# Attention and feed-forward on one core: other queues for the first loads, a table subtraction and some squares on GpSimd, other planned times

## The chip, the core and the metric

The kernel runs on one core of a Trainium2 chip. The metric is the device time of one execution in microseconds (us). A core has a matmul engine (TensorE, PE in the profile; its weight loads are PEld), an engine for elementwise work (VectorE, DVE), one for activation functions (ScalarE, ACT), GpSimd (POOL) and SyncE (SP). Each engine works through a queue of its own in order. DMAs are issued from the queues of SP, ACT or POOL.

## The reference, cut to what matters

```python
# attention: q, k, v are [8, 8, 576, 64]; bias_table is [32, 8]
scores = scale * np.matmul(q, k.transpose(0, 1, 3, 2)) + bias   # bias depends on |i - j| alone
attn = softmax(scores, axis=-1)
x = np.matmul(attn, v)            # -> [4608, 512], heads side by side
# feed-forward: w_in [512, 2048], w_out [2048, 512], alpha [2048]
h = x @ w_in
s = np.sin(alpha * h)
g = h + s * s / (alpha + 1e-09)
out = g @ w_out                   # [4608, 512]
```

## The kernel before

The work is staged by batch entry `t` (8 of them). For each `t` the heads are taken in four pairs `p`, in two groups `g` of two pairs. `plan_unit` makes a unit of scores on PE, then `exp` on ACT (line 646), and a multiplication by `exp(bias)` on DVE (lines 665 and 655), since `exp(s + b) = exp(s) exp(b)`. Far from the diagonal the bias is constant, so only a band is multiplied. `plan_av` multiplies with `v` on PE (a column of ones in `v` gives the sum of the row), DVE takes the reciprocal and normalises (lines 773 and 774), and the result is turned into `xT`.

Then comes the feed-forward on a block `b` of 512 rows, `plan_moe_in`. For each of 16 slices `f` of 128 columns: four matmuls for `h` (tag `h`, PSUM banks 0 to 5), `sin` on ACT (`sn`, line 837, into one of three buffers `s16`), the square (`sqr`, on ACT at line 844 or on another engine at line 846, into one of three buffers `sq`), and `g` on DVE (`gg`, line 851), which frees the bank of `h`. The `g` of a block are made in the order of `f`. `plan_mo` multiplies `g` by `w_out`.

The order in each engine's queue is made by a planner (`Plan`, lines 60 to 196), which runs while the program is built. A task has a cost for each engine that may take it, a priority, and an earliest time `nb`. The planner keeps one time per engine at which that engine is free, all set to `T_START` at first. At each step it finds the earliest start of each engine's candidates (line 152) and then emits, over all engines, the task with the smallest start, and among equal starts the one that ends first (line 166). A task that several engines may take thus goes where its planned start is earliest. The constants at lines 199 to 224 are what it knows of DMAs: `T_M2` and `T_MH` when the bias tables `m2r` and `mhr` may be used, `T_V` when `v` may be, `T_W` and `T_WO` when `w_in` and `w_out` may be, `T_EPS` when the product for the bias table may start. While a planned gap on PE before `WARM_END` is over 0.3 and bank 7 or 6 is free, it puts in a small matmul on zeros (`warm1`).

What is not planned is emitted in program order. Lines 467 to 499 are the opening. `tabN` (the bias table) has its last row `tabL` taken off on DVE (line 496), ACT makes `tabE = exp(tabN)`, and `plan_eps` (line 581) multiplies it with a constant on PE, copies the result to `e_sb` on DVE, and calls `loads()` in the same emission. `loads()` (line 501) emits, at once and in this order: on SP, the write of `e_sb` to `e_dram` and the loads of `v[0]`; on POOL, the reads of `m2r` and `mhr` back from `e_dram`, `w_in` mixed with the casts of `v[0]` to f16 (`cast_v`, lines 403 and 406), `q` and `k` of `t = 1`, `w_out`, the loads of `v[1]` (`v1st`), the staging of `q` and `k` of `t = 2`, and last `cast_v(1)`. No task of the plan of before has POOL among its engines, and the next POOL instruction after `cast_v(1)` is at line 378.

PSUM banks 6 and 7 serve the tags `av` and `mo`: results of `plan_av`, transposes of `q` and `k`, the product in `plan_eps`, the transpose of `alpha`, and the output blocks.

Of the kernel before, what the change touches and what calls it, by code (L numbers as in the profile page):

```python
# [13 lines left out]
ALU = mybir.AluOpType  # L14
# [186 lines left out]
QUOTA = 48  # L201
OFFSET = 0
T_START = 4.0
T_FIRST = (5.7, 6.0)
T_EPS = 6.5
T_PAIR = ((7.0, 7.6), (9.5, 11.5), (9.5, 11.5))
T_M2 = (13.0, 15.0, 17.0, 17.0)
T_MH = 14.5
T_B2 = 32.0
FILL_GAP = 0.2  # L210
NORM0 = 800
W2_PRI = 9640
SQ = {"ACT": 0.52, "DVE": 0.38}
T_V = (18.0, 52.0)
T_TR1 = (35.0, 36.5)
T_W = 29.0
T_WO = (40.0, 43.0, 46.0, 49.0)
WARM0 = 13
WARM_GAP = 0.3
# [19 lines left out]
def kernel(  # L239
# [11 lines left out]
    nc = tc.nc  # L251
    T, H, S, D = q.shape
# [48 lines left out]
    vst, vhst = [], []  # L301
# [11 lines left out]
    tabN = sgl.tile([NB, H], F32, name="tabN")  # L313
    tabL = sgl.tile([NB, H], F32, name="tabL")
# [49 lines left out]
    def stage_kq(t):  # L364
        for dst, src in ((staged_k, k), (staged_q, q)):
            nc.gpsimd.dma_start(
                out=dst.ap()[t].rearrange("s (h d) -> s h d", h=H),
                in_=src[t].rearrange("h s d -> s h d"),
            )
# [30 lines left out]
    def cast_v(t, eng, cs):  # L400
        for c in cs:
            if c < 4:
                eng.tensor_copy(out=vs[t][:, c, :, 0:D], in_=vst[t][:, c])
                continue
            z = c - 4
            eng.tensor_copy(
                out=vhs[t][64 * z : 64 * z + 64, :, VC * z : VC * z + D],
                in_=vhst[t][64 * z : 64 * z + 64],
            )

    def load_nat(dst, h0, h1, src, eng):

        eng.dma_start(out=dst, in_=src[h0:h1].rearrange("h (p i) d -> p h (i d)", i=SI))

    def load_w_in16(js):
        src = moe_w_in.rearrange("(j p) ff -> p j ff", p=128)
        for j in js:
            nc.gpsimd.dma_start(out=w_in16[:, j, :], in_=src[:, j, :])

    def load_w_out16():  # L420
        src = moe_w_out.rearrange("(f p) n -> p f n", p=128)
        for fh in range(4):
            nc.gpsimd.dma_start(
                out=w_out16[:, 4 * fh : 4 * fh + 4, :], in_=src[:, 4 * fh : 4 * fh + 4, :]
            )
# [25 lines left out]
    def load_m2r(eng, h0, h1):  # L451

        eng.dma_start(
            out=m2r[:, h0:h1],
            in_=bass.AP(tensor=e_dram, offset=EW * h0, ap=[[1, 128], [EW, h1 - h0], [1, XW]]),
        )

    def load_mhr(eng):
        for z in range(2):
            eng.dma_start(  # L460
                out=mhr[64 * z : 64 * z + 64],
                in_=bass.AP(tensor=e_dram, offset=EW * z + 192,
                            ap=[[1, 64], [2 * EW, NP], [1, 192]]),
            )

    P_ = nc.gpsimd
    P_.memset(id_sb, 1.0)
    P_.affine_select(
        out=id_sb, in_=id_sb, compare_op=ALU.is_equal, fill=0.0, base=0, pattern=[[-1, 128]],
# [6 lines left out]
        out=tabL,  # L476
        in_=bass.AP(tensor=bias_table.tensor, offset=bias_table.offset + (NB - 1) * H,
                    ap=[[0, NB], [1, H]]),
# [8 lines left out]
    vp = v[0].rearrange("h s d -> s h d")  # L487
    vq = v[0].rearrange("(hp two) s d -> two s hp d", two=2)
# [4 lines left out]
    x0 = nat0[:, 1].rearrange("s two (i d) -> s i two d", i=SI)  # L493
    nc.scalar.activation(out=natb[:, 1, :, 0], in_=x0[:, :, 0], func=AF.Copy)
    nc.vector.tensor_copy(out=natb[:, 1, :, 1], in_=x0[:, :, 1])
    nc.vector.tensor_tensor(out=tabN, in0=tabN, in1=tabL, op=ALU.subtract)
    nc.scalar.activation(out=tabE, in_=tabN, func=AF.Exp)
    warm(WARM0)
    clear(P_, 1)
# [1 line left out]
    def loads():  # L501

        nc.sync.dma_start(out=e_dram.ap(), in_=e_sb)
        for c in range(4):
            nc.sync.dma_start(out=vst[0][:, c], in_=vp[128 * c : 128 * c + 128])
        for z in range(2):
            nc.sync.dma_start(out=vhst[0][64 * z : 64 * z + 64], in_=vq[z, 512:S])
        load_m2r(P_, 0, 2)
        load_mhr(P_)
        load_m2r(P_, 2, 4)  # L510
        load_m2r(P_, 4, H)
        cast_v(0, P_, (0,))
        load_w_in16((0,))
        cast_v(0, P_, (1, 2))
        load_w_in16((1,))
        cast_v(0, P_, (3, 4, 5))
        load_w_in16((2, 3))
        for kq, src in ((0, k), (1, q)):
            load_nat(nat2[:, kq], 0, H, src[1], P_)
        load_w_out16()  # L520
        load_v32(1, P_)
        stage_kq(2)
        cast_v(1, P_, range(6))

    plan = Plan()
# [53 lines left out]
        return [x], [plan.add({"DVE": 0.25}, tail, [x], pri + 30)]  # L579

    def plan_eps():
        b, c = Buf("mo"), Cell()

        def mm(e):
            c.v = bank(b)
            full(c.v[0:H, 0:EW], tabE, phi_sb, True, True)

        def cp(e):
            copy_on(e, e_sb, c.v[0:H, 0:EW])
            loads()  # L590

        m = plan.add({"PE": 0.25}, mm, [], -900, nb=T_EPS, new=[b])
        plan.add({"DVE": 0.6}, cp, [m], -800, use=[b])

    def plan_alpha():
        b, c = Buf("mo"), Cell()
# [15 lines left out]
    def plan_unit(t, g, p, kind, c, u, ub, done, gate, base):  # L612
# [36 lines left out]
        x = plan.add({"ACT": n / 1200.0 + 0.065}, ex, [mark] + gate, base + 20, use=[b, ub])  # L649
        late = 0.0 if t else T_MH if kind == "C" else T_M2[p]  # L650
        if kind == "C":
# [87 lines left out]
    def plan_av(t, g, p, w, u, ub, done, base):  # L739
# [11 lines left out]
        for i, qc in enumerate(QS):  # L751

            def mm(e, i=i, qc=qc):
# [5 lines left out]
                for z in range(2):  # L759
                    for c in range(4):  # L760
# [4 lines left out]
            prev = [plan.add({"PE": 0.31}, mm, us + prev, base + AV_PRI + i,  # L765
                             nb=T_B2 if w == 2 else T_V[t] if t < 2 else 0.0, new=[ab] if i == 0 else [],
                             use=[ub] if i == 0 else [ub, ab])]
# [46 lines left out]
    def plan_moe_in(b, tbl):  # L814

        gcell[b], gbuf[b] = Cell(), Buf("g")
        xs = [d for (t, w), ds in xdone.items() for d in ds for q0, n in [(WIN if t else WIN0)[w]]
              if S * t + q0 < 512 * b + 512 and S * t + q0 + n > 512 * b]
        sins = []
        for f in range(NF):  # L820
            hb, sb, qb = Buf("h"), Buf("s16"), Buf("sq")
            h, s16, sq = Cell(), Cell(), Cell()

            def mm(e, f=f, h=h, hb=hb):
                h.v = bank(hb)
                x0 = 512 * b % XN
                m = min(512, XN - x0)
                for y, a, n in ((0, x0, m), (m, 0, 512 - m)):
                    if n == 0:
                        continue  # L830
                    for j in range(4):
                        full(h.v[:, y : y + n], w_in16[:, j, 128 * f : 128 * f + 128],
                             xT[:, j, a : a + n], j == 0, j == 3)

            def sn(e, f=f, h=h, s16=s16):
                s16.v = new_s16()
                nc.scalar.activation(  # L837
                    out=s16.v, in_=h.v, func=AF.Sin, scale=alphaT[:, f : f + 1]
                )

            def sqr(e, s16=s16, sq=sq):
                sq.v = new_sq()
                if e == "ACT":
                    nc.scalar.activation(out=sq.v, in_=s16.v, func=AF.Square)  # L844
                else:
                    k_of(e).tensor_tensor(out=sq.v, in0=s16.v, in1=s16.v, op=ALU.mult)  # L846

            def gg(e, f=f, h=h, sq=sq):
                if f == 0:
                    gcell[b].v = new_g()  # L850
                nc.vector.scalar_tensor_tensor(  # L851
                    out=gcell[b].v[:, f, :], in0=sq.v, scalar=inv_a[:, f : f + 1], in1=h.v,
                    op0=ALU.mult, op1=ALU.add,
                )
                if f == 0 and 1 <= b < T - 1:
                    nc.gpsimd.tensor_copy(out=tick, in_=gcell[b].v[0:1, 0, 0:1])
                    load_v16(b + 1)
                    if b + 2 < T:
                        stage_kq(b + 2)

            pri = PB + 10000 + 1000 * (b - (PB // 1000000)) + 10 * f
            m = plan.add({"PE": 4 * t_pe(512)}, mm, xs, pri, nb=T_W if b == 0 else 0.0, new=[hb])
            x = plan.add({"ACT": t_act(512) + 0.09}, sn, [m, al] + tbl, pri, new=[sb], use=[hb])
            y = plan.add(SQ, sqr, [x], pri - 5,
                         new=[qb], use=[sb])
            gdone[(b, f)] = plan.add({"DVE": 0.66}, gg, [y], pri - 6,
                                     after=[gdone[(b, f - 1)]] if f else [],
                                     new=[gbuf[b]] if f == 0 else [],
                                     use=[hb, qb] if f == 0 else [hb, qb, gbuf[b]])
            sins.append(x)  # L870
        return m, sins
# [35 lines left out]
    PB = 0  # L907
    tr = {(0, 0, kq): plan_tr(0, 0, kq, -1000, T_FIRST[kq]) for kq in range(2)}
    plan_eps()
    al = plan_alpha()  # L910
    gate, pe_gate = [], []
    for t in range(T):
# [29 lines left out]
        for b in [t] if t < T - 1 else [t, t + 1]:  # L942
            m, s_ = plan_moe_in(b, tbl)
# [36 lines left out]
```

## Time and profile before

| | us |
|---|---|
| median of three runs | 391.51 |
| lowest, highest run | 386.42, 392.5 |
| the profiled execution's own time | 388.48 |
| its span, first to last instruction | 386.7 |
| PE busy | 369.5 |
| ACT busy | 315.7 |
| DVE busy | 272.7 |
| POOL busy | 89.7 |

The profile is of one execution. Its timelines give the start of a piece of work, its length, the engine (a name that ends in q is a DMA issued from that engine's queue), the line, the operation, output and inputs, and in brackets how long the engine had stood idle before it and what released it. A line of a helper stands for all its callers: matmuls are all at line 437, copies on DVE at 535 and on ACT at 533. The 1.78 us between the span and the execution's time lie outside the profiled instructions.

### The profile page before, as it was taken

Reading aid. Unit: us, or ns where it says so; the run is one execution under the profiler, and the core shown is the slowest. Engines: PE = TensorE matmul, PEld = TensorE weight load, DVE = VectorE, ACT = ScalarE, POOL = GpSimd, SP = SyncE. Lnnn points to the kernel's source line nnn. Section 1 sums busy time; section 2 is a strip of 40 time slices with the busy share of each in tenths; the row PEclk is TensorE's granted clock in tenths of the full one; section 3 lists DMA queues with packets and bytes.
Section 4 is the critical chain, followed back from the end, with each engine's and each line's share of the span. In section 5 each row is a group of like instructions: output and inputs, shape, how many; then the busy total and the mean of one; then the engine's idle time right before and its main releaser. Section 6 shows DMA issues by size and latency. Waiting matters only on the chain.

```text
span 386.7 us, 8905 instructions
## 1 busy us (share of the span) xinstructions
PE 369.5 (96%) x3551; PEld 202.6 (52%) x3551; DVE 272.7 (71%) x614; ACT 315.7 (82%) x435; POOL 89.7 (23%) x116
## 2 busy tenths in 40 slices
PE   8568989999999999999999999999999999999995
PEld 3245544654466445686565446544667456444442
DVE  5476995759766886688677967696759676999000
ACT  4937998969997999879996999699979997998111
POOL 5773440009000280009000820073004100000000
PEclk9959999999999999999999999999999999999999
DMA  8999991289912699259915992399429812000112
GB/s 158 232 214 204 226 156 31 57 133 126 133 49 75 131 98 151 58 117 110 182 24 137 119 153 56 93 155 142 70 77 138 73 51 77 5 0 3 72 65 83
DMA packets 141946, 40.91 MB, mean 106 GB/s; under 512 B 131064, under 2 KB 136288, under 8 KB 141904
## 3 DMA queue, kind: packets, MB, share of 16 engines
q0 software_dynamic: 89904, 19.04, 55.3%
q1 hardware_dynamic: 51744, 21.00, 23.3%
q8 instruction: 28, 0.46, 0.5%
q10 hardware_dynamic: 256, 0.30, 0.3%
q14 instruction: 14, 0.11, 0.1%
HBM read 37.73 MB, written 16.52 MB: 140 GB/s over the span
## 4 chain that ended last, share of the span: by engine, by line
PE 88%; DVE 7%; DMA 3%; issue 1%; ACT 0%; DVEq 0%; ACTq 0%
PE pb L437 87%; DVE g L851 2%; DMA m2r<-e_dram 2%; DVE u L665 1%; DMA natx<-in_k_dram 1%; PE pb L798 1%; DMA e_dram<-e_sb 1%; DVE xn L774 1%; DVE kT L535 1%; DVE sq L846 1%; DVE kt L575 1%; ACT u L646 0%; DVE xT L535 0%; DVE rd L773 0%; DVE e_sb L535 0%
## 5 line engine op out<-in xcount | busy, mean ns | idle before, releaser
L646 ACT ACTIVATE u<-pb 128x1024 f16<-128x1024 f32 (+1 forms) x176 | 154.0, 966 | 15.9 <-PE pb L437 15.3
L437 PE MATMUL pb<-w_out,g 128*128 128x512 f16 x576 | 138.7, 380 | 0.0
L437 PE MATMUL pb<-xT,w_in 128*128 128x512 f16 (+4 forms) x704 | 128.0, 340 | 0.0
L837 ACT ACTIVATE s<-pb,alphaT 128x512 f16<-128x512 f32 x144 | 93.1, 681 | 14.7 <-PE pb L437 14.4
L851 DVE SCALAR_TENSOR_TENSOR g<-sq,inv_a,pb 128x512 f16<-128x512 f16 x144 | 101.5, 743 | 3.9 <-ACT sq L844 2.5
L437 PEld LDWEIGHTS <-w_in 128*128 128x128 f16 x704 | 64.0, 98 | 55.2
L665 DVE TENSOR_TENSOR u<-u,m2r 128x512 f16<-128x512 f16 (+1 forms) x128 | 61.8, 492 | 36.9 <-ACT u L646 31.3
L437 PEld LDWEIGHTS <-g 128*128 128x128 f16 x576 | 53.0, 98 | 61.4 <-issue 9.3
L437 PEld LDWEIGHTS <-u 128*128 128x128 f16 x1440 | 56.7, 99 | 16.4 <-DVE qT L535 5.2
L437 PE MATMUL pb<-v,u 128*128 128x65 f16 x1280 | 56.4, 195 | 0.0
L378 POOL COPY kt<-kT 64x256 f16<-64x256 f16 x12 | 5.5, 456 | 189.6 <-DMA kT<-staged_k 157.0
L437 PE MATMUL pb<-qT,kT 64*128 64x64 f16 (+1 forms) x512 | 43.1, 288 | 3.4 <-ACT u L646 2.6
L844 ACT ACTIVATE sq<-s 128x512 f16<-128x512 f16 x67 | 42.1, 628 | 1.1
L437 PE MATMUL pb<-vh,u 128*128 128x130 f16 x160 | 35.7, 223 | 4.9 <-DVE qT L535 4.9
L846 DVE TENSOR_TENSOR sq<-s 128x512 f16<-128x512 f16 x77 | 33.2, 436 | 10.0 <-ACT s L837 9.1
L774 DVE TENSOR_TENSOR xn<-pb,rd 128x384 f16<-128x384 f32 (+2 forms) x68 | 32.1, 471 | 2.3
L533 ACT ACTIVATE outs<-pb 128x512 f32<-128x512 f32 x15 | 9.0, 597 | 27.6 <-PE pb L437 27.6
L437 PEld LDWEIGHTS <-kT 64*128 64x128 f16 x512 | 17.0, 94 | 25.9 <-issue 18.5
L773 DVE RECIPROCAL rd<-pb 128x6 f32<-128x6 f32 (+2 forms) x68 | 12.6, 185 | 12.7 <-PE pb L437 11.6
L383 POOL DMA_DIRECT2D v<-in_v_dram x24 | 21.2, 897 | 0.1
L904 ACT ACT_TABLE_LOAD x15 | 19.2, 1283 | 0.3
L535 DVE COPY outs<-pb 128x512 f32<-128x512 f32 x21 | 14.5, 690 | 4.7 <-PE pb L437 4.7
(70 smaller groups left out, 159.5 us busy)
## 6 DMA issues: line engine op xcount, KB each, us to landing
out_dram<-outs SPq DMA_DIRECT2D x36, 256.0 KB, 2.2
staged_k<-in_k_dram POOLq DMA_DIRECT2D x6, 576.0 KB, 8.2
staged_q<-in_q_dram POOLq DMA_DIRECT2D x6, 576.0 KB, 11.2
v<-in_v_dram POOLq DMA_DIRECT2D x24, 128.0 KB, 4.9
w_in<-in_moe_w_in_dram POOLq DMA_DIRECT2D x4, 512.0 KB, 8.5
w_out<-in_moe_w_out_dram POOLq DMA_DIRECT2D x4, 512.0 KB, 18.9
w_out<-in_v_dram SPq DMA_DIRECT2D x4, 256.0 KB, 4.2
v1st<-in_v_dram POOLq DMA_DIRECT2D x4, 256.0 KB, 17.2
```

The source lines that it names most:

```text
L383: nc.gpsimd.dma_start(out=vs[t % 2][:, c, :, 0:D], in_=vp[128 * c : 128 * c + 128],)
L437: nc.tensor.matmul(out=out, lhsT=lhsT, rhs=rhs, start=start, stop=stop)
L535: k_of(e).tensor_copy(out=o, in_=i)
L646: nc.scalar.activation(out=o, in_=x, func=AF.Exp, scale=0.125)
L665: nc.vector.tensor_tensor(out=io, in0=io, in1=m2[:, 2 * p : 2 * p + 2, x0 : x0 + hi - lo], op=ALU.mult)
L773: nc.vector.reciprocal(out=r, in_=x[:, :, :, D])
L774: nc.vector.tensor_tensor(out=xn.v[:, 0:nq].rearrange("p c (z d) -> p c z d", z=2), in0=x[:, :, :, 0:D], in1=r.unsqueeze(3).to_broadcast([ ...
L837: nc.scalar.activation(out=s16.v, in_=h.v, func=AF.Sin, scale=alphaT[:, f : f + 1])
L844: nc.scalar.activation(out=sq.v, in_=s16.v, func=AF.Square)
L846: k_of(e).tensor_tensor(out=sq.v, in0=s16.v, in1=s16.v, op=ALU.mult)
L851: nc.vector.scalar_tensor_tensor(out=gcell[b].v[:, f, :], in0=sq.v, scalar=inv_a[:, f : f + 1], in1=h.v, op0=ALU.mult, op1=ALU.add,)
L904: nc.scalar.preload_act_table_set(name)
```

## The change

Four things are changed.

1. The subtraction `tabN - tabL` is made on POOL instead of DVE, at the same place in the program (ahead of `clear(P_, 1)` in POOL's queue).
2. In `loads()` the chunks 2 and 3 of `v[0]` and its two last parts (`vhst`) are loaded from POOL's queue, after `m2r(0, 2)` and `mhr` and before the other `m2r`. `w_in` is issued as two pairs, and all six casts of `v[0]` stand together between the pairs.
3. In `plan_eps` the product goes to a bank of tag `h` instead of `mo`, and the copy to `e_sb` has priority -980 instead of -800. `T_FIRST`, `T_EPS`, `T_M2`, `T_MH`, `T_V` and `T_W` have other values.
4. The squares of block 0 may go to POOL as well, with a planned cost of 1.1 beside 0.52 on ACT and 0.38 on DVE.

```diff
-T_FIRST = (5.7, 6.0)
-T_EPS = 6.5
+T_FIRST = (5.6, 6.1)
+T_EPS = 6.1
 T_PAIR = ((7.0, 7.6), (9.5, 11.5), (9.5, 11.5))
-T_M2 = (13.0, 15.0, 17.0, 17.0)
-T_MH = 14.5
+T_M2 = (14.5, 18.0, 19.5, 19.5)
+T_MH = 15.0
...
-T_V = (18.0, 52.0)
+T_V = (19.0, 50.0)
 T_TR1 = (35.0, 36.5)
-T_W = 29.0
+T_W = 30.0
...
-    nc.vector.tensor_tensor(out=tabN, in0=tabN, in1=tabL, op=ALU.subtract)
+    P_.tensor_tensor(out=tabN, in0=tabN, in1=tabL, op=ALU.subtract)
...
         nc.sync.dma_start(out=e_dram.ap(), in_=e_sb)
-        for c in range(4):
+        for c in range(2):
             nc.sync.dma_start(out=vst[0][:, c], in_=vp[128 * c : 128 * c + 128])
-        for z in range(2):
-            nc.sync.dma_start(out=vhst[0][64 * z : 64 * z + 64], in_=vq[z, 512:S])
         load_m2r(P_, 0, 2)
         load_mhr(P_)
+        for c in range(2, 4):
+            P_.dma_start(out=vst[0][:, c], in_=vp[128 * c : 128 * c + 128])
+        for z in range(2):
+            P_.dma_start(out=vhst[0][64 * z : 64 * z + 64], in_=vq[z, 512:S])
         load_m2r(P_, 2, 4)
         load_m2r(P_, 4, H)
-        cast_v(0, P_, (0,))
-        load_w_in16((0,))
-        cast_v(0, P_, (1, 2))
-        load_w_in16((1,))
-        cast_v(0, P_, (3, 4, 5))
+        load_w_in16((0, 1))
+        cast_v(0, P_, range(6))
         load_w_in16((2, 3))
...
-        b, c = Buf("mo"), Cell()
+        b, c = Buf("h"), Cell()
...
         m = plan.add({"PE": 0.25}, mm, [], -900, nb=T_EPS, new=[b])
-        plan.add({"DVE": 0.6}, cp, [m], -800, use=[b])
+        plan.add({"DVE": 0.68}, cp, [m], -980, use=[b])
...
-            y = plan.add(SQ, sqr, [x], pri - 5,
+            y = plan.add({**SQ, "POOL": 1.1} if b == 0 else SQ, sqr, [x], pri - 5,
```

## The prediction

> **What bounds the kernel now.** I read the page first, its busy shares and its 40 slices (9.7 us each).
>
> ```profile
> PE 369.5 (96%) x3551; PEld 202.6 (52%) x3551; DVE 272.7 (71%) x614; ACT 315.7 (82%) x435; POOL 89.7 (23%) x116
> ...
> PE   8568989999999999999999999999999999999995
> ...
> POOL 5773440009000280009000820073004100000000
> PEclk9959999999999999999999999999999999999999
> ```
>
> From the seventh slice on PE is full. Only the opening, some 60 us, holds idle PE, and there POOL is busiest. So a shift of the moment at which PE becomes full moves the end by as much. The chain that ended last says where that moment is:
>
> ```profile
> 57.78 0.09 DVE kt L575
> 57.87 0.01 issue
> 57.88 0.18 DVE kt L575
> 58.06 0.03 issue
> 58.09 0.76 DVE g L851
> 58.85 0.04 issue
> 58.90 19.13 PE pb L437 x227
> ```
>
> Before 58.85 the chain runs on DVE through the `g` of block 0; after it, on PE nearly to the end. Hence I need the end of block 0 (58.85) in the changed kernel. Next, the timeline of DVE and ACT in block 0:
>
> ```profile
> 38.80 0.63 ACT L844 ACTIVATE sq<-s 128x512 f16<-128x512 f16 x1
> ...
> 39.34 1.25 ACT L837 ACTIVATE s<-pb,alphaT 128x512 f16<-128x512 f32 x2
> ...
> 40.48 0.63 ACT L844 ACTIVATE sq<-s 128x512 f16<-128x512 f16 x1
> ...
> 40.62 0.43 DVE L846 TENSOR_TENSOR sq<-s 128x512 f16<-128x512 f16 x1
> 41.14 0.75 DVE L851 SCALAR_TENSOR_TENSOR g<-sq,inv_a,pb 128x512 f16<-128x512 f16 x1
> ```
>
> The `g` at 41.14 is that of f = 2; its square ran on ACT at 40.48, after two sines in a row. Last, the timeline of POOL's queue:
>
> ```profile
> 36.75 0.88 POOL L395 DMA_DIRECT2D v1st<-in_v_dram  x1 [2.03 <-DMA nat<-in_q_dram]
> 39.28 0.64 POOL L398 DMA_DIRECT2D v1st<-in_v_dram  x1 [1.65 <-DMA w_out<-in_moe_w_out_dram]
> 41.80 0.62 POOL L398 DMA_DIRECT2D v1st<-in_v_dram  x1 [1.88 <-DMA w_out<-in_moe_w_out_dram]
> 44.88 2.22 POOL L366 DMA_DIRECT2D staged_k<-in_k_dram  x1 [2.46 <-DMA w_out<-in_moe_w_out_dram]
> 47.03 2.29 POOL L366 DMA_DIRECT2D staged_q<-in_q_dram  x1
> 49.37 2.68 POOL L403 CAST v<-v1st 128x512 f16<-128x512 f32 x4
> 52.00 0.86 POOL L406 CAST vh<-v1st 64x256 f16<-64x256 f32 x2
> 85.15 0.85 POOL L378 COPY kt<-kT 64x256 f16<-64x256 f16 x2 [32.30 <-PE pb L437]
> ```
>
> POOL issues the list of `loads()` in program order and stands at DMA issues until earlier transfers land. Counted along the queue, each waiting issue is released by the DMA eight places ahead of it. The list ends at 52.00 + 0.86 = 52.86. It was emitted when `e_sb` was planned, so whatever the planner puts on POOL for block 0 comes behind it.
>
> **The change, part by part.**
>
> *Subtraction, bank and priority.* The table lands at 1.27 + 4.4 = 5.67 by its DMA row; DVE subtracts at 6.08. On POOL it runs at about 5.7, and the clears behind it (4.22 to 6.65, 2.43 us) end near 8.3, covered by POOL's wait until 11.16 for `e_dram`. The product on PE at 7.02 had waited for the kT copy, which held its bank; from a bank of `h` it follows the transposes that end near 6.72. Priority -980 is ahead of the `kt` copies (-970), so `e_sb` moves from 7.42 to about 7.1 and the first `m2r` issue from 11.16 to about 10.85: -0.3 us, between 0 and -0.6.
>
> *Split loads.* SP loses four DMAs. POOL gets two chunks of v at 0.89 and two parts at 0.63 (the `v1st` rows): 3.04 us, which move the issue of `m2r(2,4)` from 13.11 to about 15.9. The first `m2r` landed at 17.38, 6.2 us after its issue, and between 12 and 13 the hardware queue moved 0.25 of the 0.26 MB. With half of v gone I expect it near 15, and DVE's first bias product there instead of at 17.47; the later `m2r` near 20 to 21, as before (19.9 and 21.0). Six casts in one piece (4 x 0.64 + 2 x 0.56 = 3.7 us) begin behind two more issues, near 18.5, and end near 22.3 instead of 20.22. Queued behind them are `w_in` 2 and 3 (20.16 to about 22.3), nat2 and w_out; `w_in` was complete near 31, for a first use at 36.16, so 5 us cover that. Waiting for the casts is the first product with v on PE, which began at 22.65 once the qT copy at the end of DVE's bias products had freed its bank: now about 22.4. With `T_V` at 19 one more unit of scores may go ahead of it, one exp (0.97) of the 5.36 us in which ACT stood idle from 19.7 to 25.07. Opening together: -1.0 us, between -2.5 and +1.
>
> The Trainium skill speaks against much from the split: "Trainium Kernel Development and Optimization", Key Constraints, says that the queues of SP, ACT and POOL share the same 16 DMA engines, so that other queues only save issue time. By it this part would be 0 instead of -1.0; the 263 GB/s in the microsecond from 12 agree, since only the order of landings changes.
>
> *Squares.* The planner knows POOL as free from 4.0 on, as no `loads()` instruction is a planned task. By its own costs, from the start of the first sine: sine 1 runs 0.86 to 1.43, square 1 is ready at 1.61 and goes to ACT (equal start, earlier end); sines 2 and 3 follow on ACT (2.13 to 2.70, 2.70 to 3.27). Square 2 is ready at 2.88. ACT could start it at 3.27, DVE at 2.97 (behind `g` 1), POOL at 2.88: it goes to POOL. The traced order above (two sines, then the square on ACT) is this place. More follow, I guess five to eight of 16.
>
> On the chip that square waits until 52.86. Behind it: the `g` of f = 2, and with it all later `g`, norms and copies in DVE's queue; on ACT sine 5, as three `s16` buffers are held; on PE `h` 8, as the six banks are; then `xT`, the transposes of t = 1, `plan_mo`. All stop from about 41 to 54.
>
> The cost: the trace of before has no POOL product. Its nearest row is POOL's 128x512 cast with one input, 0.64; with two inputs at most twice that, 1.3. I take 1.0, nearer the doubled row since there are two inputs. (The "GPSIMD Engine Reference", section 3.1, gives 2.6 cycles per element at 1.2 GHz for two inputs: an estimate of 1.11 us, by which the sum would be 0.1 more; its section 4.1 advises VectorE for elementwise work.) So `g` 2 starts at 52.86 + 1.0 + about 0.15 for two hand-overs = 54.0. From that `g` to the end DVE took 58.85 - 41.14 = 17.7 us with almost no idle time. Off this come 1.8 for two `kt` copies that took 2.15 beside POOL's staging issue (0.36 elsewhere), which is over by then, and half of DVE's four later squares (1.36 + 0.75, so 1.05) that POOL may take. Left: 14.9. Block 0 ends at 68.9, 10.1 later than 58.85. The opening's -1.0 counts nothing here: it is spent waiting for POOL.
>
> Bounds: POOL's end 1.5 us either way, since one queue carries the same bytes in another order; the square 0.65 to 1.3; the rest 13.8 (all four squares gone) to 17.7 (nothing saved). That makes +7.1 to +14.6. PE may run at half clock after the stall: after the idle time from 17.8 the granted clock was 0.50 until 28.25, 5.6 us into the new work. That costs PE up to 2.8 us in a stretch that DVE bounds; I take 0, as it lies inside the upper bound.
>
> *Sum.* Span 386.7 + 10.1 = 396.8; with the 1.78 outside it, 398.6, against the execution's own 388.48. The median of the runs is 3.03 above that execution. I go halfway, since either may be the usual run: 398.6 + 1.5, about 400.
>
> **The rivals.**
>
> *Squares reach POOL late (0.10).* If other work on the planned DVE and ACT shifts so that the first POOL square is f = 6 (its `g` at 45.43), the rest is 13.4 - 1.8 - 1.05 = 10.6, the end 64.6, +5.8; for f = 8, about +3.4. Time 392 to 397. Against it: ACT alternates sine and square from 41.0 on, so squares were already waiting at f = 4.
>
> *No square waits: not slower (0.15).* One mechanism: the first POOL square stands where POOL is already free. It decides at f = 11, whose `g` ran at 53.99; from there on nothing is lost. Then the opening's -1.0 stays, and up to 1 us of squares leaves ACT and DVE: 388.48 - 1.5 = 387.0, or 388.5 halfway to the median; 384 to 390 with the opening's ends. For it: block 0 is slow in its second half. Against it: the hand plan above.
>
> *POOL gets even later (0.05).* If the four added issues lengthen POOL's list by their 3.04 us instead of hiding in its DMA waits, 400 becomes 403, at most 409. Against it: from 25 to 45 each issue waits for a landing, not for POOL.
>
> **How the numbers follow.** The stall has 0.70, with 394 to 406 as its own range (+7.1 on 388.48 less 1.5 for scatter; +14.6 and the median's 3.0). 391 to 406 holds nearly all of it, most of the late squares and half of the last rival: about 0.8. Two per cent, about what a measurement of this kernel can tell from no change, is 7.8 us: some 0.62 of the stall and 0.05 of the last rival are above it, so slower 0.67. The late squares, the stall's low end and most of the second rival are within it: 0.30. Faster by 7.8 us would need nearly all the idle PE of the opening: 0.03.
>
> **What would show it.** Right: in POOL's queue products at L846 directly behind the cast of `vh` near 53, an idle DVE of over 10 us ahead of an early `g` L851 released by POOL, low PEclk near 50, a last `g` of block 0 near 69, and the later 326.7 us unchanged. The opening's steps: `m2r` landing near 15, casts ending near 22.3. Wrong: products on POOL before 50, or no gap on DVE between 40 and 54; or a stall caught up after 70 by a PE that had work to do meanwhile.

## The result and the profile after

The changed kernel takes 401.15 us (median of six runs, 399.67 to 401.88) beside 392.0 us for the kernel before in the same runs (386.42 to 393.56). The ratio is 1.029, with a 95% interval of 1.022 to 1.035: slower. The profiled execution took 401.2 us with a span of 399.5. Ratios here leave out executions that took over 1.5% longer than the fastest of the same kernel, so they can differ from the quotient of two medians.

From the page of the changed kernel, its 40 slices (10.0 us each):

```profile
PE   8889239999999999999999999999999999999996
...
DVE  4777048675977697769766886688668866899100
...
PEclk9869759999999999999999999999999999999999
```

The fifth slice, from 40 to 50 us, is new: DVE does next to nothing in it and PE little. In the sixth the granted clock of PE is half. From the seventh on PE is full, as before. Now POOL's timeline:

```profile
45.96 2.23 POOL L366 DMA_DIRECT2D staged_k<-in_k_dram  x1 [2.51 <-DMA w_out<-in_moe_w_out_dram]
...
53.27 0.86 POOL L406 CAST vh<-v1st 64x256 f16<-64x256 f32 x2
54.22 1.03 POOL L845 TENSOR_TENSOR sq<-s 128x512 f16<-128x512 f16 x1
58.98 1.03 POOL L845 TENSOR_TENSOR sq<-s 128x512 f16<-128x512 f16 x1 [3.73 <-DVE g L850]
64.16 1.04 POOL L845 TENSOR_TENSOR sq<-s 128x512 f16<-128x512 f16 x1 [4.14 <-DVE kT L534]
66.62 1.04 POOL L845 TENSOR_TENSOR sq<-s 128x512 f16<-128x512 f16 x1 [1.42 <-ACT s L836]
69.14 1.04 POOL L845 TENSOR_TENSOR sq<-s 128x512 f16<-128x512 f16 x1 [1.48 <-ACT s L836]
```

Five squares (f = 2, 7, 10, 12, 14) stand behind the last cast of `loads()`. The first starts without any wait in front of it: its sine had ended nearly 16 us earlier, but the queue only got there at 54.22. Only the first square costs; for the others POOL waits, not the others for POOL. DVE's timeline in the same stretch:

```profile
39.86 0.29 DVE L773 TENSOR_TENSOR xn<-pb,rd 128x128 f16<-128x128 f32 x1
55.29 0.75 DVE L850 SCALAR_TENSOR_TENSOR g<-sq,inv_a,pb 128x512 f16<-128x512 f16 x1 [15.14 <-POOL sq L845]
...
70.44 1.40 DVE L850 SCALAR_TENSOR_TENSOR g<-sq,inv_a,pb 128x512 f16<-128x512 f16 x2
```

DVE stands for 15.14 us ahead of the `g` of f = 2, released by the square on POOL, and the last `g` of block 0 ends at 71.84 instead of 58.85: 13.0 us later, against 12.8 us in the span. The chain that ended last goes through the same place:

```profile
53.72 0.42 POOL vh L406
54.14 0.08 issue
54.22 1.04 POOL sq L845
55.29 0.76 DVE g L850
56.04 0.04 issue
56.09 1.87 PE pb L437 x4
57.95 0.11 PE pb L797
58.06 1.71 PE pb L437 x4
```

After the first `g` it runs on PE at half clock: four matmuls take 1.87 and 1.71 us on it, while four took 1.03 in block 0 before the stall.

### The profile page after: what moved, and what is told of

The parts are those of the page before. It is cut to its first block, busy times and chain, and to the rows that moved or that the text cites. A ratio compares the mean times of both kernels' runs of the same rounds, so it can differ in the third digit from the quotient of the medians.

```text
span 399.5 us, 8920 instructions
## 1 busy us (share of the span) xinstructions
PE 374.4 (94%) x3557; PEld 204.9 (51%) x3557; DVE 271.1 (68%) x610; ACT 314.8 (79%) x433; POOL 97.5 (24%) x126
## 4 chain that ended last, share of the span: by engine, by line
PE 86%; DMA 8%; POOL 4%; DVE 1%; issue 0%; ACT 0%; ACTq 0%; DVEq 0%
PE pb L437 85%; DMA v1st<-in_v_dram 4%; DMA nat<-in_q_dram 4%; PE pb L551 1%; POOL v L403 1%; PE pb L797 1%; POOL m2r L453 1%; POOL w_in L418 1%; POOL vh L406 0%; POOL w_out L509 0%; DMA e_dram<-e_sb 0%; POOL mhr L460 0%; POOL w_out L511 0%; POOL sq L845 0%; POOL nat L413 0%
## 5 line engine op out<-in xcount | busy, mean ns | idle before, releaser
L437 PE MATMUL pb<-xT,w_in 128*128 128x512 f16 (+4 forms) x704 | 129.9, 343 | 14.0 <-DVE g L850 14.0
L845 DVE TENSOR_TENSOR sq<-s 128x512 f16<-128x512 f16 x73 | 31.4, 434 | 9.7 <-ACT s L836 9.1
L534 DVE COPY outs<-pb 128x512 f32<-128x512 f32 x21 | 14.5, 689 | 3.9 <-PE pb L437 3.9
```

Of the source, the lines that this page charges most:

```text
L437: nc.tensor.matmul(out=out, lhsT=lhsT, rhs=rhs, start=start, stop=stop)
L534: k_of(e).tensor_copy(out=o, in_=i)
```

## The experiments

All ratios are to the kernel before, run beside it on the same chip. Medians in us.

| run | this | before | ratio (95%) |
|---|---|---|---|
| e1, change without POOL squares | 385.44 | 389.01 | 0.990 (0.986 to 0.993) |
| e2, POOL squares alone | 403.53 | 389.01 | 1.032 (1.026 to 1.039) |
| e3, only f = 2 on POOL | 401.32 | 389.01 | 1.030 (1.026 to 1.035) |
| e4, only f = 8 on POOL | 395.36 | 389.01 | 1.015 (1.010 to 1.020) |
| e5, bias part of the opening | 389.09 | 391.5 | 1.000 (0.996 to 1.004) |
| e6, split loads | 387.68 | 391.5 | 0.994 (0.991 to 0.998) |
| e7, planned times | 391.8 | 391.5 | 0.992 (0.987 to 0.997) |
| e8, split loads and times | 386.23 | 391.5 | 0.988 (0.983 to 0.992) |
| e9, POOL's list shortened | 386.67 | 391.52 | 0.990 (0.985 to 0.995) |
| e10, planner told | 390.22 | 391.52 | 1.001 (0.997 to 1.005) |
| e11, as e9, loads held back | 384.25 | 392.12 | 0.983 (0.978 to 0.989) |
| e12, e1 once more | 385.56 | 392.12 | 0.987 (0.982 to 0.993) |

**The squares: e1 and e2.** e1 takes the fourth part out of the change; e2 puts it alone into the kernel before.

```diff
-            y = plan.add({**SQ, "POOL": 1.1} if b == 0 else SQ, sqr, [x], pri - 5,
+            y = plan.add(SQ, sqr, [x], pri - 5,
```

> The change without its fourth part: no square of block 0 may go to POOL. Theory (squares stand behind POOL's load list): the 15 us gap of DVE ahead of the g of f = 2 is gone, block 0 begins at 34.5 as in the changed kernel instead of 36.2, and the time is 392.0 - 1.6 = about 390.4. Rival A (a POOL square is dear in itself, through its length, its hand-over or its hold on DVE): the same 390.4, since no square is left on POOL. Rival B (the other order of the loads makes the loss): still near 401.

> The kernel of before with the fourth part alone: squares of block 0 may go to POOL, loads and planned times as before. Theory: POOL's list ends at 52.9 as in the profile of before, the g of f = 2 starts near 54.0, block 0 ends 16.5 later near 70.5 instead of 58.9, so 392.0 + 11.7 = about 403.7. Rival A: also slower, but without one long gap: many short waits of DVE on POOL. Rival B: 392, no change.

Without the squares the change is faster than the kernel before, by 1.0% (0.7 to 1.4%); with them alone the kernel before becomes 3.2% slower. So the whole loss comes from the squares, and rival B (the loads) falls. e1 gained more than the expected 1.6 us, 3.6 between medians; that is followed up below.

**One square is enough: e3 and e4.** The others go to ACT or DVE; the square of f = 2, or of f = 8 in e4, must go to POOL.

```diff
-            y = plan.add({**SQ, "POOL": 1.1} if b == 0 else SQ, sqr, [x], pri - 5,
+            y = plan.add({"POOL": 1.1} if (b, f) == (0, 2) else SQ, sqr, [x], pri - 5,
```

> The change, but of the squares of block 0 only that of f = 2 goes to POOL (it must); the others go to ACT or DVE. Theory: one square is enough, as it alone cannot start before POOL's list ends near 54.1: g of f = 2 near 55.3, then some 16.5 to 17.5 us, so 400 to 402.5. Rival A (a cost for each square): a fifth of the whole loss of about 10.7 beside the kernel without POOL squares, so about 392.6.

> As the run before, but the one square on POOL is that of f = 8. Theory: DVE runs freely up to g of f = 7, then waits for POOL until about 55.3, and the last eight g take the 9.3 us that they took before: block 0 ends near 64.6 instead of 57.2, so 390.4 + 7.4 = about 397.8, between the run with f = 2 and the run with none. Rival A: the same as with f = 2, about 392.6.

A line of DVE's timeline in each, e3 first:

```profile
54.87 0.75 DVE L850 SCALAR_TENSOR_TENSOR g<-sq,inv_a,pb 128x512 f16<-128x512 f16 x1 [14.84 <-POOL sq L845]
```

```profile
55.68 1.41 DVE L850 SCALAR_TENSOR_TENSOR g<-sq,inv_a,pb 128x512 f16<-128x512 f16 x2 [8.16 <-POOL sq L845]
```

One square costs as much as five. A square six places later costs 8.16 us of DVE's time instead of 14.84, and both waits end at the same moment, about 55, when POOL's list is through. A price for each square (rival A, 392.6 for both) is excluded. e4 came out at +9.9 us over e1 where +7.4 was expected: block 0 ended at 65.92 in e4 and at 56.84 in e1, 9.1 apart, since the last eight `g` took 10.2 us after the wait instead of 9.3, the wait ended 0.4 us later and e1 was faster than assumed. The longer rest runs on PE, which after the wait makes eight products with `w_in` at half clock (1.90 us at full clock):

```profile
58.43 3.59 PE L437 MATMUL pb<-xT,w_in 128*128 128x512 f16 x8
```

e2's median lies 0.2 us from the 403.7 worked out for it, but by luck. Over the kernel before beside it the loss is 14.5 us instead of 11.7. In its profiled execution POOL's list ended at 58.75 instead of 52.9: v of t = 0 landed late, its last cast ran at 26.53 instead of 19.69, and all that stands behind it in POOL's queue moved along. The end of the list is thus itself a matter of the opening.

**Is a POOL square dear when POOL is free? e9 and e11.** In e9 the loads of v of t = 1 go to SP's queue, and its casts and the staging of t = 2 are emitted behind the last `g` of block 0. The squares stay on POOL.

```diff
-        load_v32(1, P_)
-        stage_kq(2)
-        cast_v(1, P_, range(6))
...
+                if b == 0 and f == 0:
+                    load_v32(1, nc.sync)
+                if b == 0 and f == NF - 1:
+                    cast_v(1, P_, range(6))
+                    stage_kq(2)
```

> The whole change with its POOL squares, but POOL's list is cut short: v of t = 1 is loaded from SP's queue when g of f = 0 is planned, and its casts and the staging of t = 2 are emitted behind g of f = 15. So POOL's list ends with w_out near 27 and squares can run when their sine is ready. Theory: no gap of DVE on POOL over 1.5 us, DVE and ACT are relieved of five squares, time at or up to 2 us below the change without POOL squares, 383 to 386 beside 389 for the kernel before (ratio 0.985 to 0.99). Rival A (a POOL square is dear in itself): DVE waits some 0.5 to 1 us at each of five squares, 387 to 391.

POOL's timeline in e9: the squares start right behind their sines, and no `g` waits for POOL in the whole of block 0.

```profile
40.30 1.04 POOL L842 TENSOR_TENSOR sq<-s 128x512 f16<-128x512 f16 x1 [9.46 <-ACT s L833]
45.84 1.04 POOL L842 TENSOR_TENSOR sq<-s 128x512 f16<-128x512 f16 x1 [4.50 <-ACT s L833]
```

The stall is gone with the squares still there, so it is the queue and not the square. But the opening was late, first product with `w_in` at 36.36, and SP's queue says why:

```profile
9.10 1.04 SPq L505 DMA_DIRECT2D w_out<-in_v_dram  x2
10.18 5.64 SPq L395 DMA_DIRECT2D v1st<-in_v_dram  x4
15.86 2.76 SPq L398 DMA_DIRECT2D v1st<-in_v_dram  x2
```

SP has nothing to wait for and issues the loads for t = 1 in the middle of the opening, though they are emitted with block 0. The casts of `v[0]` began 1.7 us later than in e1, behind an issue of `w_in` that waited 1.50 us for `mhr` to land; then they waited 1.0 us for their chunks, and ended at 23.75 instead of 21.1 (e1). So the time, 386.67, lies above the 383 to 386 that were expected. e11 holds the loads back by a small write of POOL into their buffer, behind the issues of `w_out`.

```diff
         load_w_out16()
+        P_.memset(v1st[:, 0:2], 0.0)
```

> As the run with the shortened list, but a small POOL write into the buffer of v of t = 1, emitted behind the issues of w_out, holds SP's six loads back until about 27 (in that run SP had issued them from 10.2 on, in the middle of the opening). Theory: the opening is again that of the change without POOL squares (first product with w_in near 33.3 instead of 36.4) and block 0 keeps its 21.1 us with POOL squares instead of 23.6 without: 1.5 to 3 us below the change without POOL squares in the same call, about 383 beside 389 to 391 for the kernel before. Rival: the loads of v of t = 1 now share the DMA engines with w_in and w_out, and w_in comes late: no gain, 385 to 387.

> The change without its POOL squares once more, on the same chip as the run above, for a comparison. Theory and rival: 0.99 of the kernel before, as in the first run of it.

e11 has the lowest median here, 1.7% below the kernel before (1.1 to 2.2%). Block 0, from the first product with `w_in` to the end of the last `g`, took 21.05 us (32.22 to 53.27), against 21.58 in e12 and 23.56 in e1. But e1 and e12 are one kernel: the 2.0 us between them lie in DVE's copies into `kt` (two pairs took 2.65 and 0.50 us in e1, 0.41 and 0.74 in e12). The 1.5 to 3 us expected of e11 rested on e1's 23.56; 1.3 came. Whether the squares on POOL bring anything over e12 stays open: the medians differ by 1.3 us, but the intervals overlap, and e11 also moves the casts and the staging out of block 0. Its first product with `w_in` came 1.6 us earlier than in e12 as well, ahead of any square, with PE's granted clock back at 1.00 from 19.3 on instead of 24.5.

**Telling the planner: e10.** The planner's time of POOL starts at 48, some 6 us short of the list's real end. It then chose f = 12 and 14.

```diff
         free = {e: t0 for e in ("PE", "ACT", "DVE", "POOL", "SP")}
+        free["POOL"] = T_POOL
...
+T_POOL = 48.0
```

> The whole change, but the planner starts POOL's time at 48 instead of 4: then the squares of f = 12 and 14 alone go to POOL. Theory: POOL's list ends near 54.7 and the first square near 55.8, while g of f = 12 ran at 52.4 without POOL squares: a wait of some 3 us less two saved squares, so 2 to 3 us above the change without POOL squares, near 388 beside 389 for the kernel before (ratio about 0.997). Rival A: two fifths of the loss of five squares, some 6 us above it, near 392.

Lines of the timeline of DVE and of PE, and a row of the stretches (its length, PE busy, PEld, DVE, ACT, POOL, granted clock, DMA share, GB/s):

```profile
55.05 0.75 DVE L852 SCALAR_TENSOR_TENSOR g<-sq,inv_a,pb 128x512 f16<-128x512 f16 x1 [2.46 <-POOL sq L847]
```

```profile
56.52 3.08 PE L439 MATMUL pb<-w_out,g 128*128 128x512 f16 x9 [3.26 <-DVE kT L536]
...
60.93 1.25 PE L439 MATMUL pb<-w_out,g 128*128 128x512 f16 x5
```

```profile
58.00:59.00 1.00, 1.00 (x4) 0.30 (x2) 0.84 (x2) 0.00 (x0) 0.00 (x0) 0.50 1.48 94
```

The wait was 2.46 us, near the 3 expected, but the loss against e1 is 4.3 us (1.001 less 0.990 of 391) instead of 2 to 3. After its 3.26 us without work PE makes nine matmuls in 3.08 us, 0.34 each; later five take 1.25, 0.25 each. The granted clock is 0.50 in the row between them. Here, as in e4, a wait in block 0 is paid a second time through PE's clock. The planner's times also are not the chip's: POOL's list ended at 53.9 here, but 48 in planned time already lies behind most of block 0; on the chip `g` of f = 12 then had to wait.

**Where the opening's gain comes from: e5 to e8.** Each puts a part of the opening alone into the kernel before, without POOL squares: e5 the subtraction, the bank, the priority, `T_FIRST` and `T_EPS`; e6 the new `loads()`; e7 the other planned times; e8 the parts of e6 and e7 together. The edits are those lines of the diff above.

> Part of the opening alone: the kernel of before with the subtraction on POOL, the product in a bank of h and the new T_FIRST, T_EPS and priority; loads and the other times as before, no square on POOL. Theory P (each part of the opening brings its own share, as the prediction summed them): -0.3 us. Theory Q (the parts work only together, since the order planned by the new times needs the new landings): 0 to -0.3 us.

> The kernel of before with the other split of the loads alone, planned times as before, no square on POOL. Theory P: m2r lands near 15 and the bias products begin there, the casts end near 21.4; some -1 us. Theory Q: PE still stands at its first product with v, which now waits for the casts, with the next scores behind it, so 0 to -0.5 us.

> The kernel of before with the new T_M2, T_MH, T_V and T_W alone, loads as before, no square on POOL. Theory P (the later planned time of the first product with v puts one or two units of scores ahead of it, and the copies of q ahead of the first bias product): -1.5 to -2.5 us, most of the gain of the opening. Theory Q: the bias products still wait for m2r until 17.4, so -0.5 us or less.

> The kernel of before with split loads and the new T_M2, T_MH, T_V and T_W, but without the part at the bias table, no square on POOL. Theory P: the sum of the two runs before this. Theory Q: more than that sum, close to the 4.0 us that the change brings without POOL squares.

The bias part alone shows no gain in the ratio; the mean of all its runs is 389.6 beside 391.1 us, so a small gain is not excluded. The split loads bring 0.6%, more than either theory gave them; with the times it is 1.2%, as much as the whole change without squares (1.0 and 1.3%). e7 is unclear: its runs lie between 385.3 and 393.7, and its median is no lower than that of before. So theories P and Q are not told apart by the sum, but the load split is shown to help by itself. What can hold the bias part back is seen in POOL's and PE's timelines of e5, which has the loads of before; the profiled execution, 391.28 us, is among its longest:

```profile
22.44 0.39 POOL L406 CAST vh<-w_out 64x256 f16<-64x256 f32 x1 [3.71 <-DMA w_out<-in_v_dram]
25.63 0.40 POOL L406 CAST vh<-w_out 64x256 f16<-64x256 f32 x1 [2.80 <-DMA w_out<-in_v_dram]
```

```profile
26.09 0.27 PE L437 MATMUL pb<-vh,u 128*128 128x130 f16 x1 [7.90 <-POOL vh L406]
```

The bias products began at 15.07 instead of 17.47, but PE stood for 7.90 us until the last part of v had landed and was cast. The DMA issues of `vhst` in e5 and in the profile of before (KB each, median us from issue to landing), e5 first:

```profile
w_out<-in_v_dram SPq DMA_DIRECT2D x2, 64.0 KB, 11.8
```

```profile
w_out<-in_v_dram SPq DMA_DIRECT2D x2, 64.0 KB, 7.0
```

The same loads from the same queue landed 4.8 us later in this execution. The profiles of e2 and e7, which have the loads of before too, give 11.6 and 13.6, with PE waiting 8.11 and 9.00 us for the cast. So of four executions the profile of before is the one in which v came early: its 388.48 lies in the lower part of the runs of before, which reach from 386 to 394 over all series. With split loads and the new times PE waits 1.17 us for the same cast in e1 and 2.98 in e12, and the runs lie close: 384.7 to 386.3 in both. In e6, with the old times, they still reach 392.8, so the loads alone do not end the scatter. That late landings of v make the scatter of before is argued from these four executions, not shown.

## Why the prediction was right, point by point

*The bound.* Right: PE's row after block 0 is unchanged, and the shift of block 0 (13.0) is the shift of the span (12.8). Behind block 0 the span has 327.9 us before (386.7 - 58.85; the 326.7 that I wrote is a slip) and 327.7 after.

*The mechanism.* Right in its path: f = 2 was the first square on POOL, as the hand plan had it; five went there (guessed five to eight); DVE, ACT and PE stood from about 41 to 55. Two details were wrong. ACT still made sine 5 (40.67) and stopped at its square, released by the `g` of f = 2; and PE stopped one slice earlier, at `h` 7 instead of `h` 8, so that more of its work lay behind the stall.

*The sizes.*

| term | predicted | measured |
|---|---|---|
| end of POOL's list | 52.86 | 54.13 |
| square on POOL | 1.0 | 1.03 |
| `g` of f = 2 starts | 54.0 | 55.29 |
| from there to the end of block 0 | 14.9 | 16.55 |
| block 0 ends | 68.9 | 71.84 |
| span | 396.8 | 399.5 |
| time | 400 | 401.15 |

The list ended 1.3 us later, mostly because the staging was released at 45.96 instead of 44.88; one cast of v of t = 1 also waited 0.52 us for its chunk. This was inside the bound of 1.5. The rest of block 0 was 1.65 us too short in the sum. The failed step is the 0 that I put for PE's clock: I called it covered by DVE, but the chain above runs on PE at half clock. None of DVE's four later squares was left on DVE, where I had taken off half; so DVE's own sum was 13.8, and the stretch on PE cost 2.7 us more. Half of the 5.2 us at half clock is 2.6: by this estimate the clock accounts for nearly all of it, though no run takes the half clock out. The rows of the changed kernel by stretch (its length, PE busy, PEld, DVE, ACT, POOL, granted clock, DMA share, GB/s) end the half clock near 61.3, 5.2 us after PE took up work:

```profile
54.00:60.00 6.00, 3.92 (x16) 1.47 (x17) 4.21 (x10) 2.84 (x6) 2.19 (x3) 0.50 1.89 122
```

```profile
60.50:61.00 0.50, 0.50 (x13) 0.38 (x10) 0.46 (x1) 0.50 (x2) 0.00 (x0) 0.50 0.00 0
61.00:61.50 0.50, 0.50 (x2) 0.13 (x3) 0.50 (x2) 0.50 (x2) 0.00 (x0) 0.71 0.04 16
61.50:62.00 0.50, 0.50 (x4) 0.24 (x3) 0.50 (x2) 0.19 (x1) 0.00 (x0) 1.00 0.00 0
```

The "GPSIMD Engine Reference", section 3.1, which gave an estimate of 1.11 us for the square, was 0.08 above the measured 1.03; my 1.0, between the cast's row and its double, was 0.03 below.

*The opening.* The steps of the split came as predicted (first `m2r` products at 15.54 for "near 15"; casts of `v[0]` ended at 21.40 for 22.3; the first product with v came at 21.45 for 22.4, with one more unit of scores ahead of it). The step ahead of them did not: `e_sb` came at 7.87 instead of 7.1, behind products on zeros that took longer, and the first `m2r` was issued at 10.29 all the same, as the write to `e_dram` held it for 1.7 us from its issue instead of 3.0. The size was wrong: -1.0 us, at most -2.5, against 3.6 us between the medians of e1 and before, and 6.6 in e12. The 0 that stood beside it for the split was further off, as e6 gained 0.6% by the split alone.

Two steps of the opening's sum failed. The old loads were priced by one execution that had them early. And the sum has no term for PE's clock in the opening: the granted clock stayed at 0.50 until 28.3 in the profile of before, 27.2 in that of the changed kernel, 24.5 in e12 and 23.8 in e1. In the same order the first product with `w_in` came at 36.16, 34.54, 33.83 and 33.28, so 1.6 to 2.9 us earlier even beside the execution with early loads, while the first product with v differs by only 0.5 us among the last three. What the clock is worth by itself no run shows. Between the two profiles none of it reached the end, as predicted: it went into the wait for POOL. Where v lands late, as in e2, POOL's list ends later too, and then the opening does count.

*The median.* Going halfway between the profiled execution and the median of before was a guess. By luck it cancelled part of the missing 2.7 us of the span.

*The rivals.* Late squares are a real course, as e4 shows, and dearer than the +3.4 us that I gave for f = 8: 395.36 - 389.01 = 6.4 over the kernel before. In e4's profile the `g` of f = 8 started at 55.68 instead of 54.0, and the rest took 10.2 us instead of 8.25 with PE at half clock. The rival without a wait would have needed a POOL list that ends before block 0 begins; e9 and e11 make one. A later list from the four added issues did not come, apart from the 1.3 us.

## What to carry to other kernels

An engine that a planner sees as idle may have a full queue of unplanned work: before a task is allowed on it, read from its timeline when the queue ends, and where the first such task will stand in it. One task in an in-order queue behind such a list costs as much as five, and an idle PE after it pays again at half clock. And a term that rests on the landing of a DMA should be taken from several executions: here the one profile had the last loads of v nearly 5 us and more earlier than three other executions of the same loads.

## What the runs showed of the hardware that was not expected

The 13 products on zeros at the start of each kernel took 4.50 us in the profile of before and 5.63 in that of the changed kernel, with the same instructions and a granted clock of 1.00 in both. The first ones start 0.43 us apart; the change to a faster pace came at 4.22 in one and after 5.9 in the other. "TensorE: Matmul & The Clock Gate", Part 1, says that PE runs at half rate until it has been busy for one window of about 3.4 us, and that the window runs freely, so that the moment varies from execution to execution. The runs agree that it varies: e1 and e12 are one kernel, and there the same products took 5.68 and 4.33 us, the latter the shortest of all 14 profiles (4.33 to 5.73). They do not agree with the length, as the change at 4.22 comes 3.0 us after the first product, less than one such window. The row PEclk did not show the slow pace. The difference did not reach the end of the opening: the first product with `w_in` came at 33.28 in e1 and 33.83 in e12.

DVE's pairs of small copies into `kt` took 2.15 us in the profile of before, 2.65 in e1 and 2.06 in e10 where POOL was issuing the staging DMAs, each ending within 0.2 us of the issue of `staged_q`; where POOL stood idle they took 0.35 or 0.36. Beside the same issues in e12 two pairs took only 0.41 and 0.74, so it is not the rule. In e11 the square of f = 3 on DVE ran beside the square on POOL (36.16 to 37.19) and took 0.79 instead of 0.42, as it did in e9:

```profile
36.68 0.79 DVE L843 TENSOR_TENSOR sq<-s 128x512 f16<-128x512 f16 x1
```

"SBUF — State Buffer", Who interferes with whom, says that a DVE instruction with two inputs in SBUF and a POOL instruction that reads SBUF exclude each other; the 0.37 us more lie within the 0.51 us for which the two overlap. That section's point on DMAs issued from POOL is the other way round: there DVE holds up the issue, while here the issue went with a DVE copy that was held up. It also says that the order of issue decides which of the two waits; no run here tests that.
